# Linear attention and a gated feed-forward layer on one core: the first batch's q, v and all weights loaded in one row by GpSimd, and ScalarE's side work moved behind the output evictions

## The chip, the cores and the metric

The kernel runs on one core of a Trainium2 chip. Its time is the device time in microseconds, as the median of several runs: 335.98 before the change (3 runs, 335.76 to 336.26). One execution was taken with the hardware profiler; all times inside the kernel are from that one and count from the start of its span.

## The reference

Eight batches, eight heads, 576 positions, head size 64. First an attention without softmax: relu of q and k, each times a cosine and a sine of the position, so that the feature size doubles to 128; kv is the sum over positions of k's features times v, z the sum of k's features; the output is q's features times kv, divided by q's features times z.

```python
def phi(x, c, s):
    r = np.maximum(x, 0.0)
    return np.concatenate([r * c, r * s], axis=-1)
kv = np.einsum('bhsf,bhsd->bhfd', phi(k), v)
z = np.sum(phi(k), axis=2)
num = np.einsum('bhsf,bhfd->bhsd', phi(q), kv)
den = np.einsum('bhsf,bhf->bhs', phi(q), z)[..., None] + 1e-06
x = (num / den)             # laid out as 4608 tokens of 512
xn = x / sqrt(mean(x * x) + 1e-06) * rms_g
out = (silu(xn @ w_gate) * (xn @ w_val)) @ w_out     # 512 -> 1536 -> 512
```

Inputs and output are float32.

## The kernel before

**Tiles.** A batch's 576 positions are four tiles of 128 and half a tile; the half tiles of two batches make one tile. So there are nine blocks of 512 tokens: block b is the four full tiles of batch b, block 8 the four shared tiles. In a block the feed-forward runs in twelve steps (`step`, L626): in each, TensorE makes one bank of gate products (`gps`) and one of value products (`vps`), ScalarE takes silu of the first (`sil`, L647), VectorE multiplies (`hT`, L653). In blocks 0 to 4 a step takes fewer columns of more weight tiles, so that it can start before all four tiles of the block are there. From block 2 on each step also runs four of the 48 output matmuls of the block before (`out_mm`, L438): twelve of them fill the single bank `acc`, so that every third step ends with ScalarE's copy of that bank to SBUF (`osb`, L452) and two stores on SP's queue. Block 0's output matmuls are spread through `lead` (L663), between block 0 and block 1, where batch 1's attention is prepared.

**Attention work** is laid between the steps by a plan written by hand: `at(g, slot, function)` puts a piece into a slot of step g, and `step` runs the slots in the order sp, act0, dve0, gate matmuls, mid, value matmuls, silu, act1, dve1, product, output matmuls, pe. Every engine runs its instructions in program order, so a slot fixes what stands ahead of what on each engine's queue. The chain for one tile is: features of q and k (`feat`, L226, on DVE or ACT), a turn of q's features (`q_turn`, L281, a DMA transpose on SP, or on TensorE by `q_turn_pe` with an eviction `rqT`), `kv_mm` (L262) with its eviction `kvm`, `num_mm` (L309), `divide` (L335: three operations on DVE), `sumsq` (L353: a square with a sum on ACT, then the power -1/2 on GpSimd, `rs`, L361), `norm` (L364, `xn`, DVE), and a turn of `xn` into `xnT`, on TensorE by `x_turn_pe` (L380) with the eviction `x_evict` (L387).

**The opening**, before block 0, is written out at L722 to L763 and runs this chain for batch 0, with dummy matmuls (`warm_up`) between. A load of a tensor of a batch (`load`, L92) is two DMAs, of the even and the odd partitions; `cuts` splits it by columns. Batch 0's loads all go on SP's queue, in the order k, q(0:2), v(0:2), v(2:5), the norm's weights gb, q(2:5). The weights go on GpSimd's queue, which converts them to bf16: `load_gv(c)` loads a third of w_gate and w_val, `load_wo(c)` a third of w_out. Ahead of the first of them stands `pool_after` (L222), a copy on GpSimd of one element of v's first cast, so that the queue goes on only when that cast is done. The third `load_gv` comes later in the opening; `more_loads` (L516), in step 3, issues w_out and the k, q and v of batches 1 and 2, all on GpSimd's queue. GpSimd also computes each tile's `rs`, in order with its DMA issues.

```python
def load(t, src, b, odd_five=False, cuts=(0, NC5)):
    if b == 0:
        eng = nc.sync
    else:
        eng = nc.scalar if b > 2 and src is not v else nc.gpsimd
```

Of the kernel before, what the change touches and what calls it, by code (L numbers as in the profile page):

```python
# [11 lines left out]
BF16 = mybir.dt.bfloat16  # L12
# [5 lines left out]
def kernel(  # L18
# [11 lines left out]
    nc = tc.nc  # L30
    B, H, S, D = q.shape
    DM = H * D
    DFF = moe_w_gate.shape[1]
    P = 128
# [6 lines left out]
    NC5 = J + 1  # L41
# [5 lines left out]
    def K(i):  # L47
        tc.keep_in_program_order(i)
        return i

    consts = ctx.enter_context(tc.tile_pool(name="consts", bufs=1))
# [31 lines left out]
    def lanes(odd_five):  # L83

        if odd_five:
            return ((0, 0, J), (1, J, NC5))
        return ((1, NC5, J), (0, 0, NC5))

    def load(t, src, b, odd_five=False, cuts=(0, NC5)):  # L92
        if b == 0:
            eng = nc.sync
        else:
            eng = nc.scalar if b > 2 and src is not v else nc.gpsimd
        for lo, hi in zip(cuts[:-1], cuts[1:]):
            for par, t0, jn in lanes(odd_five):
                z = min(hi, jn)
                K(eng.dma_start(  # L100
                    out=t[par:P:2, :, lo * D : z * D],
                    in_=src[b, :, :, :].rearrange("h (i j) d -> i h (j d)", j=NT)[
                        :, :, (t0 + lo) * D : (t0 + z) * D
                    ],
                ))

    def load_v(b, cuts=(0, NC5)):
        load(vraw[b], v, b, False, cuts)

    def load_k(b):  # L110
        load(kraw[b], k, b)

    def load_q(b, cuts=(0, NC5)):
        load(qraw[b], q, b, b % 2 == 1, cuts)
# [3 lines left out]
    clear_fifth(v0, nc.vector)  # L118
    gb = consts.tile([P, DM], FP32, name="gb")
    load_k(0)  # L120
    load_q(0, (0, 2))
    load_v(0, (0, 2, NC5))
    K(nc.sync.dma_start(
        out=gb[:, :], in_=moe_rms_g.rearrange("(o d) -> o d", o=1).to_broadcast([P, DM])
    ))
    load_q(0, (2, NC5))


    iota_i = consts.tile([P, 1], mybir.dt.int32, name="iota_i")
# [1 line left out]
    odd_i = consts.tile([P, 1], mybir.dt.int32, name="odd_i")  # L131
    row_i = consts.tile([P, J], mybir.dt.int32, name="row_i")
    nc.gpsimd.iota(row_i[:, :], pattern=[[1, J]], base=0, channel_multiplier=0)
    iota_f = consts.tile([P, 1], FP32, name="iota_f")
    odd_f = consts.tile([P, 1], FP32, name="odd_f")
    row_f = consts.tile([P, J], FP32, name="row_f")
# [2 lines left out]
        out=odd_i[:, :], in_=iota_i[:, :], scalar=1, op=ALU.bitwise_and  # L139
# [10 lines left out]
        out=iota_f[:, :], in0=iota_f[:, :], scalar1=J + 0.5, scalar2=None, op0=ALU.mult  # L150
    )
    for u, half in ((0, 0.5), (1, -0.5)):
        nc.vector.scalar_tensor_tensor(
            out=first[:, u : u + 1], in0=odd_f[:, :], scalar=half, in1=iota_f[:, :],
# [3 lines left out]
            out=th[:, 1, u * J : (u + 1) * J], in0=row_f[:, :],  # L158
# [3 lines left out]
        out=th[:, 1, 2 * J : NT], in0=first[:, 1:2],  # L162
# [3 lines left out]
        out=th[:, 0, :], in_=th[:, 1, :], scalar=math.pi / 2.0, op=ALU.add  # L166
# [7 lines left out]

    ident_b = consts.tile([P, P], BF16, name="ident_b")
    masks.make_identity(nc, ident_b[:, :])
    mhalf = consts.tile([P, 1], FP32, name="mhalf")
    nc.gpsimd.memset(mhalf[:, :], -0.5)

# [5 lines left out]
    vx = [consts.tile([P, H, E], BF16, name=f"vx{j}") for j in range(NC5)]  # L185
# [15 lines left out]
    wg = consts.tile([P, NDT, DFF], BF16, name="wg")  # L201
    wv = consts.tile([P, NDT, DFF], BF16, name="wv")
    wo = consts.tile([P, NNT, DM], BF16, name="wo")
    probe = consts.tile([1, 1], BF16, name="probe")
    NG = 3
    GC = DFF // NG
    n4 = NNT // NG
# [1 line left out]
    def load_gv(c):  # L209
        for (w, src) in ((wg, moe_w_gate), (wv, moe_w_val)):  # L210
            K(nc.gpsimd.dma_start(
                out=w[:, :, c * GC : (c + 1) * GC],
                in_=src[:, c * GC : (c + 1) * GC].rearrange("(t p) n -> p t n", p=P),
            ))

    def load_wo(c):
        K(nc.gpsimd.dma_start(
            out=wo[:, c * n4 : (c + 1) * n4, :],
            in_=moe_w_out[c * n4 * P : (c + 1) * n4 * P, :].rearrange("(t p) m -> p t m", p=P),
        ))  # L220

    def pool_after(src):  # L222
        K(nc.gpsimd.tensor_copy(out=probe[:, :], in_=src))


    def feat(dst, src, scale, act):  # L226
# [99 lines left out]
    def xn_block(blk):  # L326
        if blk not in xnT:
            tag = "xnT" if blk < B else "xnTr"
            pool = xntp if blk < B else consts
            xnT[blk] = pool.tile([P, NDT, TB], BF16, name=tag, tag=tag)  # L330
        return xnT[blk]
# [55 lines left out]
    def x_evict(key, blk, col, dve=False):  # L387
        dst, src = xn_block(blk)[:, :, col * P : (col + 1) * P], xps.pop(key)[:, :, :]
        if dve:
            K(nc.vector.tensor_copy(out=dst, in_=src))  # L390
        else:
            K(nc.scalar.copy(out=dst, in_=src))  # L392
# [37 lines left out]
    def out_store(blk, jt, osb):  # L430
        if blk < B:
            rows = list(out_rows(blk, jt))
        else:
            rows = [r for o in range(2) for r in out_rows(2 * jt + o, J)]
        for par, dst in rows:
            K(nc.sync.dma_start(out=dst, in_=osb[par:P:2, :]))

    def out_mm(blk, i, tail=False):  # L438

        jt, nn = divmod(i, NNT)  # L440
        if nn == 0:
            if tail and jt % 2 == 0:
                acc[blk] = ps_gv.tile([P, DM], FP32, name="acc2", tag="gv")
            else:
                acc[blk] = ps_acc.tile([P, DM], FP32, name="acc", tag="acc")
        K(nc.tensor.matmul(  # L446
            acc[blk][:, :], lhsT=hT[blk][:, nn, jt * P : (jt + 1) * P], rhs=wo[:, nn, :],
            start=(nn == 0), stop=(nn == NNT - 1),
        ))
        if nn == NNT - 1:  # L450
            osb = osbp.tile([P, DM], FP32, name="osb", tag="osb")
            K(nc.scalar.copy(out=osb[:, :], in_=acc[blk][:, :]))  # L452
            out_store(blk, jt, osb)
# [6 lines left out]
    def at(g, w, f, *a):  # L460
        plan[g, w].append(lambda: f(*a))
# [13 lines left out]
    def feat_at(g, f, b, j, act):  # L475
        for c in range(2):
            on_act = c == 1 and act
            at(g, "act1" if on_act else "dve0" if f == k_feat else "dve1", f, b, j, c, on_act)

    def q_at(g, b, t, act=False):  # L480
        feat_at(g, q_feat, b, t, act)
        if t < J:
            at(g, "dve1", q_turn, b, t)

    def k_at(g, b, j, act=False):
        feat_at(g, k_feat, b, j, act)
# [26 lines left out]
        at(3, "dve1", q_feat, 0, J, c)  # L513


    def more_loads():  # L516
        for c in range(NG):
            load_wo(c)
        load_k(1)
        load_q(1, (0, 2))  # L520
        load_v(1)
        load_q(1, (2, NC5))
        load_k(2)
        load_q(2)
        load_v(2)

    at(3, "pe", more_loads)

    def pe_tile_at(g, key, xblk, col, gx):

# [7 lines left out]
    def q2_at(g, b, t):  # L538
        for c in range(2):
            at(g, "act1" if c else "dve1", q_feat, b, t, c, c == 1)  # L540
        if t < J:
            at(g, "dve1", q_turn, b, t)


    at(12, "dve0", divide, (1, 2))
# [64 lines left out]
    def run(g, w):  # L610
        for f in plan[g, w]:
            f()
# [13 lines left out]
    def step(blk, nn):  # L626
        g = blk * NNT + nn
        run(g, "sp")
        run(g, "act0")
        run(g, "dve0")  # L630
        while late_turns:
            x_turn(*late_turns.pop(0))
        if nn == 0:
            hT[blk] = htp.tile([P, NNT, TB], BF16, name="hT", tag="hT")
        if blk in PARTS:
            n0, c0, cn = PARTS[blk][nn]
            ni = TB // cn
            gp = gv_mm_part(wg, "gps", blk, n0, c0, cn)
            run(g, "mid")
            vp = gv_mm_part(wv, "vps", blk, n0, c0, cn)  # L640
            dst = hT[blk][:, n0 : n0 + ni, c0 : c0 + cn]
        else:
            gp = gv_mm(wg, "gps", blk, nn)
            vp = gv_mm(wv, "vps", blk, nn)
            dst = hT[blk][:, nn, :]
        sil = silp.tile([P, TB], BF16, name="sil", tag="sil")
        K(nc.scalar.activation(out=sil[:, :], in_=gp[:, :], func=AF.Silu))  # L647
        run(g, "act1")
        run(g, "dve1")
        a, c = vp[:, :], sil[:, :]  # L650
        if blk in PARTS:
            a, c = (z.rearrange("p (i n) -> p i n", i=ni) for z in (a, c))
        K(nc.vector.tensor_tensor(out=dst, in0=a, in1=c, op=ALU.mult))  # L653
        if blk > 1:
            for i in range(4 * nn, 4 * nn + 4):
                out_mm(blk - 1, i)
        run(g, "pe")

    def outs(lo, hi):
# [74 lines left out]
    for j in range(NC5):  # L734
        v_cast(0, j, act=(j == 3))
        kv_mm(0, j, j == 0, j == NC5 - 1)
        if j == 0:
            pool_after(vx[0][0:1, 0, 0:1])
            load_gv(0)
            load_gv(1)  # L740
        if j == 1:
            warm_up(5)
    kv_evict(0)
# [13 lines left out]
    num_mm((0, 2))  # L757
    q_feat(0, 3, 0, act=True)
    x_turn_pe((0, 0))
    x_evict((0, 0), 0, 0)  # L760
    load_gv(2)
    divide((0, 2))
    norm((0, 1))  # L763

# [55 lines left out]
```

## Time and profile before

| | us | |
|---|---|---|
| median of the runs | 335.98 | 335.76 to 336.26 |
| the profiled execution | 337.09 | its time as a run |
| its span | 334.9 | first to last instruction |
| TensorE busy (matmul) | 318.3 | 95% of the span |
| VectorE (DVE) busy | 190.2 | 57% |
| ScalarE (ACT) busy | 169.2 | 51% |
| GpSimd (POOL) busy | 47.9 | 14% |
| gate and value matmuls of the feed-forward start | 20.3 | first `gps` |
| DMA | 50.63 MB | mean 151 GB/s |

The chain that ended last is TensorE for 80% of the span and DMA for 7%. The granted TensorE clock is full in every slice but the last. The GB/s count what is written to the destination; weights and v of batches 1 to 7 are read as float32 and written as bf16, so they read twice what they show.

To read a line of the timeline: start, duration, engine, source line, operation, the tile written and the tiles read, the shape, how many were merged, and in brackets how long the engine had stood idle and what released it. PEld is TensorE's weight load; SPq, ACTq and POOLq are DMA issues by these engines.

### The profile page before, as it was taken

The page shows a single profiled execution, that of the slowest core. Times are in us where ns is not written, and L with a number is a line of the kernel's source. Part 1 is how long each engine was busy: PE and PEld are TensorE (multiplying, and loading weights), DVE is VectorE, ACT ScalarE, POOL GpSimd, SP SyncE. Part 2 cuts the span into 40 slices and gives each one's busy share as a digit, 9 for nine tenths or more (in the row PEclk, how much of TensorE's full clock was granted, in tenths as well). Part 3 has the DMA queues.
Part 4 walks back from the last instruction along what each step waited for, and adds up shares of the span by engine and source line. Part 5 has one row for each costly group of instructions (what it writes and reads, how often), then busy time and mean ns, then how long its engine had stood idle before and what let it go on. Part 6 is the DMA issues. An engine that isn't in the chain of part 4 may idle for free.

```text
span 334.9 us, 7537 instructions
## 1 busy us (share of the span) xinstructions
PE 318.3 (95%) x3009; PEld 213.4 (64%) x3045; DVE 190.2 (57%) x394; ACT 169.2 (51%) x320; POOL 47.9 (14%) x91
## 2 busy tenths in 40 slices
PE   6679999998999999999999999999999999999995
PEld 4568856996887788778877744454444444444443
DVE  5676476776866575588857686665652422222300
ACT  3764377775875447486646474644433322233221
POOL 3446361300012120031103001000100000000000
PEclk9999999999999999999999999999999999999999
DMA  7999999893239989999969994253123021000012
GB/s 219 273 205 184 229 296 348 228 234 95 65 96 197 239 202 169 283 272 202 167 120 237 291 165 110 65 142 80 47 65 94 32 65 46 34 33 31 31 63 96
DMA packets 82147, 50.63 MB, mean 151 GB/s; under 512 B 49056, under 2 KB 76464, under 8 KB 82112
## 3 DMA queue, kind: packets, MB, share of 16 engines
q1 hardware_dynamic: 58032, 24.65, 33.8%
q0 software_dynamic: 13360, 13.57, 22.7%
q10 hardware_dynamic: 10720, 11.93, 12.2%
q8 instruction: 24, 0.39, 0.5%
q14 instruction: 11, 0.09, 0.1%
HBM read 38.01 MB, written 9.44 MB: 142 GB/s over the span
## 4 chain that ended last, share of the span: by engine, by line
PE 80%; DMA 7%; DVE 5%; ACT 4%; issue 2%; ACTq 1%; POOL 1%; SPq 0%; DVEq 0%
PE acc L446 25%; PE gps L401 12%; PE vps L401 12%; PE gps L414 12%; PE vps L414 12%; DMA rqT<-qp 3%; PE att L316 3%; DMA wv<-in_moe_w_val_dram 3%; PE att L267 2%; DMA kbuf<-in_k_dram 2%; DVE kp L231 1%; ACT kp L229 1%; PE qtp L294 1%; DVE xn L366 1%; PE acc L781 1%
## 5 line engine op out<-in xcount | busy, mean ns | idle before, releaser
L653 DVE TENSOR_TENSOR hT<-vps,sil 128x512 bf16<-128x512 f32 x108 | 74.5, 690 | 98.9 <-PE vps L401 59.6
L647 ACT ACTIVATE sil<-gps 128x512 bf16<-128x512 f32 x108 | 64.5, 597 | 109.6 <-PE gps L401 61.9
L446 PE MATMUL acc<-wo,hT 128*128 128x512 bf16 x395 | 101.8, 379 | 1.9 <-ACT osb L452 0.6
L446 PEld LDWEIGHTS <-hT 128*128 128x128 bf16 x420 | 40.0, 98 | 40.5 <-issue 0.9
L414 PE MATMUL gps<-xnT,wg 128*128 128x128 bf16 (+1 forms) x704 | 62.7, 239 | 0.7 <-ACT xnT L392 0.7
L414 PE MATMUL vps<-xnT,wv 128*128 128x128 bf16 (+1 forms) x704 | 62.8, 239 | 0.5 <-DMA wv<-in_moe_w_val_dram 0.5
L414 PEld LDWEIGHTS <-wg 128*128 128x128 bf16 x704 | 50.2, 98 | 6.8 <-DMA wg<-in_moe_w_gate_dram 0.6
L414 PEld LDWEIGHTS <-wv 128*128 128x128 bf16 x704 | 51.3, 98 | 3.8 <-DMA wv<-in_moe_w_val_dram 0.7
L361 POOL TENSOR_TENSOR rs<-ss,mhalf 128x1 f32<-128x1 f32 x36 | 20.1, 559 | 200.1 <-ACT sq L356 200.0
L401 PE MATMUL gps<-xnT,wg 128*128 128x512 bf16 x139 | 36.7, 379 | 0.4
L401 PE MATMUL vps<-xnT,wv 128*128 128x512 bf16 x141 | 36.5, 379 | 0.1
L452 ACT COPY osb<-acc 128x512 f32<-128x512 f32 x35 | 20.4, 583 | 26.4 <-PE acc L446 21.8
L401 PEld LDWEIGHTS <-wv 128*128 128x128 bf16 x192 | 18.8, 98 | 22.7
L366 DVE SCALAR_TENSOR_TENSOR xn<-x,rs,gb 128x512 bf16<-128x512 f32 x36 | 26.9, 748 | 8.8 <-POOL rs L361 8.8
L401 PEld LDWEIGHTS <-wg 128*128 128x128 bf16 x192 | 18.0, 98 | 20.1
L345 DVE TENSOR_TENSOR x<-att,rec 128x512 f32<-128x512 f32 x36 | 24.9, 691 | 1.2
L231 DVE TENSOR_SCALAR kp<-kbuf,trig 128x512 bf16<-128x512 f32 x50 | 22.8, 489 | 3.1 <-DMA kbuf<-in_k_dram 2.7
L231 DVE TENSOR_SCALAR qp<-qbuf,trig 128x512 bf16<-128x512 f32 x52 | 23.9, 485 | 0.4 <-DMA qbuf<-in_q_dram 0.4
L356 ACT ACTIVATE sq<-x 128x513 f32<-128x513 f32 x36 | 22.6, 626 | 2.9 <-DVE x L345 2.5
L229 ACT ACTIVATE kp<-kbuf,trig 128x512 bf16<-128x512 f32 x30 | 20.6, 712 | 3.4 <-DMA kbuf<-in_k_dram 3.4
L316 PEld LDWEIGHTS <-rqT 128*128 128x128 bf16 x320 | 14.3, 98 | 9.1 <-issue 1.1
L229 ACT ACTIVATE qp<-qbuf,trig 128x512 bf16<-128x512 f32 x28 | 19.6, 714 | 0.4 <-DMA qbuf<-in_q_dram 0.4
(63 smaller groups left out, 193.2 us busy)
## 6 DMA issues: line engine op xcount, KB each, us to landing
out_dram<-osb SPq DMA_DIRECT2D x70, 128.0 KB, 2.6
kbuf<-in_k_dram ACTq DMA_DIRECT2D x5, 640.0 KB, 6.1
qbuf<-in_q_dram ACTq DMA_DIRECT2D x5, 640.0 KB, 8.2
kbuf<-in_k_dram ACTq DMA_DIRECT2D x5, 512.0 KB, 4.8
qbuf<-in_q_dram ACTq DMA_DIRECT2D x5, 512.0 KB, 6.5
vbuf<-in_v_dram POOLq DMA_DIRECT2D x7, 320.0 KB, 9.4
vbuf<-in_v_dram POOLq DMA_DIRECT2D x7, 256.0 KB, 6.7
wg<-in_moe_w_gate_dram POOLq DMA_DIRECT2D x3, 512.0 KB, 10.1
```

The source lines that it names most:

```text
L229: K(nc.scalar.activation(out=dst, in_=src, func=AF.Relu, scale=scale))
L231: K(nc.vector.tensor_scalar(out=dst, in0=src, scalar1=scale, scalar2=0.0, op0=ALU.mult, op1=ALU.max,))
L316: K(nc.tensor.matmul(nums[key][:, h // Z, (h % Z) * E : (h % Z) * E + D + 1], lhsT=rqT[a, t][:, h, :], rhs=kvm[a % NK][:, h, 0 : D + 1], s ...
L345: K(nc.vector.tensor_tensor(out=x[:, 0:DM].rearrange("p (z s d) -> p z s d", z=2, d=D), in0=a[:, :, :, 0:D], in1=r.unsqueeze(3).to_broadca ...
L356: K(nc.scalar.activation(out=sq[:, :], in_=xs[key][:, :], func=AF.Square, scale=1.0 / math.sqrt(DM), accum_out=ss[:, :],))
L366: K(nc.vector.scalar_tensor_tensor(out=xn[:, :], in0=xs.pop(key)[:, 0:DM], scalar=rss.pop(key)[:, :], in1=gb[:, :], op0=ALU.mult, op1=ALU. ...
L401: K(nc.tensor.matmul(ps[:, :], lhsT=w[:, dt, nn * P : (nn + 1) * P], rhs=xnT[blk][:, dt, :], start=(dt == 0), stop=(dt == NDT - 1),))
L414: K(nc.tensor.matmul(ps[:, i * cn : (i + 1) * cn], lhsT=w[:, dt, (n0 + i) * P : (n0 + i + 1) * P], rhs=xnT[blk][:, dt, c0 : c0 + cn], star ...
L446: K(nc.tensor.matmul(acc[blk][:, :], lhsT=hT[blk][:, nn, jt * P : (jt + 1) * P], rhs=wo[:, nn, :], start=(nn == 0), stop=(nn == NNT - 1),))
L452: K(nc.scalar.copy(out=osb[:, :], in_=acc[blk][:, :]))
L647: K(nc.scalar.activation(out=sil[:, :], in_=gp[:, :], func=AF.Silu))
L653: K(nc.vector.tensor_tensor(out=dst, in0=a, in1=c, op=ALU.mult))
```

## The change

Four things:

- Batch 0's q and v and the norm's weights gb go to GpSimd's queue; only k stays on SP's. On GpSimd's queue the order is q(0:2) after two iotas, v after the identity matrix, then (behind the other constants) q(2:5), gb, all three thirds of w_gate and w_val and two thirds of w_out. The copy that held the queue back is gone.
- The last third of w_out and batch 1's k are issued in step 0, batch 1's q and v in step 2, batch 2's in step 3.
- In the steps from block 2 on that end with an output eviction, ACT's slot act1 runs after the output matmuls and their eviction, not ahead of them. So that a turn of q by DMA still follows its features in program order, these turns move from slot dve1 to slot pe.
- The eviction of the first turned tile of the opening, `x_evict((0, 0), 0, 0)`, goes from ACT to DVE.

```diff
     def load(t, src, b, odd_five=False, cuts=(0, NC5)):
-        if b == 0:
+        if b == 0 and src is k:
             eng = nc.sync
         else:
             eng = nc.scalar if b > 2 and src is not v else nc.gpsimd
...
     load_k(0)
-    load_q(0, (0, 2))
-    load_v(0, (0, 2, NC5))
-    K(nc.sync.dma_start(
-        out=gb[:, :], in_=moe_rms_g.rearrange("(o d) -> o d", o=1).to_broadcast([P, DM])
-    ))
-    load_q(0, (2, NC5))
...
     nc.gpsimd.iota(row_i[:, :], pattern=[[1, J]], base=0, channel_multiplier=0)
+    load_q(0, (0, 2))
...
     masks.make_identity(nc, ident_b[:, :])
+    load_v(0, (0, 2, NC5))
...
-    def pool_after(src):
-        K(nc.gpsimd.tensor_copy(out=probe[:, :], in_=src))
+    load_q(0, (2, NC5))
+    K(nc.gpsimd.dma_start(
+        out=gb[:, :], in_=moe_rms_g.rearrange("(o d) -> o d", o=1).to_broadcast([P, DM])
+    ))
+    for c in range(NG):
+        load_gv(c)
+    for c in range(2):
+        load_wo(c)
...
     def q_at(g, b, t, act=False):
         feat_at(g, q_feat, b, t, act)
         if t < J:
-            at(g, "dve1", q_turn, b, t)
+            at(g, "pe", q_turn, b, t)
...
-    def more_loads():
-        for c in range(NG):
-            load_wo(c)
-        load_k(1)
-        load_q(1, (0, 2))
-        load_v(1)
-        load_q(1, (2, NC5))
-        load_k(2)
-        load_q(2)
-        load_v(2)
-
-    at(3, "pe", more_loads)
+    at(0, "pe", load_wo, 2)
+    at(0, "pe", load_k, 1)
+    for f, *a in ((load_q, 1, (0, 2)), (load_v, 1), (load_q, 1, (2, NC5))):
+        at(2, "pe", f, *a)
+    for f in (load_k, load_q, load_v):
+        at(3, "pe", f, 2)
...
     def q2_at(g, b, t):
         for c in range(2):
             at(g, "act1" if c else "dve1", q_feat, b, t, c, c == 1)
         if t < J:
-            at(g, "dve1", q_turn, b, t)
+            at(g, "pe", q_turn, b, t)
...
         K(nc.scalar.activation(out=sil[:, :], in_=gp[:, :], func=AF.Silu))
-        run(g, "act1")
+        ends = blk > 1 and nn % 3 == 2
+        if not ends:
+            run(g, "act1")
         run(g, "dve1")
...
                 out_mm(blk - 1, i)
+        if ends:
+            run(g, "act1")
         run(g, "pe")
...
-        if j == 0:
-            pool_after(vx[0][0:1, 0, 0:1])
-            load_gv(0)
-            load_gv(1)
...
     x_turn_pe((0, 0))
-    x_evict((0, 0), 0, 0)
-    load_gv(2)
+    x_evict((0, 0), 0, 0, dve=True)
     divide((0, 2))
     norm((0, 1))
```

More of the change, by code (lines that the diff above doesn't have):

```diff
@@ L203 @@
     wo = consts.tile([P, NNT, DM], BF16, name="wo")
-    probe = consts.tile([1, 1], BF16, name="probe")
     NG = 3
```

## The prediction

> **What bounds the kernel now.** I read the busy shares first, then TensorE's waits by stretch, then the timeline of the places where it waits. Times are us from the span's start, in one profiled execution: span 334.9, time 337.09. The median is 335.98, so 1.11 lower than that execution; I work out a difference from the trace and apply it to the median. A timeline line gives start, duration, engine, line, operation and tiles; in brackets the idle time before it and what ended that.
>
> ```profile
> PE 318.3 (95%) x3009; PEld 213.4 (64%) x3045; DVE 190.2 (57%) x394; ACT 169.2 (51%) x320; POOL 47.9 (14%) x91
> ```
>
> TensorE is the bound. The change can win only where TensorE idles, or where the opening delays its stream. The waits view from 84 us on shows one releaser for TensorE, two output evictions of 0.6 us together; the larger is
>
> ```profile
> 140.70 1.02 PE L446 MATMUL acc<-wo,hT 128*128 128x512 bf16 x4 [0.38 <-ACT osb L452]
> ```
>
> From 60 to 84 it idles 1.5 us (a DMA transpose, a norm): neither the transposes' issue step there nor the loads beside them move. From 44 to 60 it idles 0.85 us, in the lead to block 1. The rest is the opening: the first gate matmuls start at 20.30.
>
> ```profile
> 1.56 5.61 DMA kbuf<-in_k_dram
> 12.96 1.01 DVE L243 CAST vx<-v 128x512 bf16<-128x512 f32 x2 [0.43 <-DMA v<-in_v_dram]
> 19.67 0.58 ACT L392 COPY xnT<-xps 128x512 bf16<-128x512 bf16 x1 [0.29 <-PE xps L384]
> 20.13 0.74 DVE L366 SCALAR_TENSOR_TENSOR xn<-x,rs,gb 128x512 bf16<-128x512 f32 x1
> 20.30 1.05 PE L414 MATMUL gps<-xnT,wg 128*128 128x128 bf16 x16 [0.67 <-ACT xnT L392]
> 22.06 1.07 PE L414 MATMUL vps<-xnT,wv 128*128 128x128 bf16 x16 [0.48 <-DMA wv<-in_moe_w_val_dram]
> ```
>
> k lands at 1.56 + 5.61 = 7.17; from there a chain of features, turns, casts, kv, num, divide, sumsq and norm runs with one DMA wait, 0.43 for v, until xnT is evicted at 20.25. The weights are late only for the first vps, by 0.48. So the gate costs half a microsecond, not the 12 us it stands for.
>
> **The change, part by part.**
>
> *Loads of q and v to GpSimd's queue.* k's two DMAs keep their issue times (0.74, 1.56). In the trace's single-packet records SP's q and v go in packets of 512 bytes at 291 GB/s (8 to 10 us); GpSimd's loads of the same form (q, k of batches 1 and 2) go in packets of about 4096 bytes at 351 (49 to 51 us). q(0:2) and v are 0.52 + 1.18 = 1.70 MB: 5.8 us at the one rate, 4.9 at the other, so v lands about 0.9 earlier and the 0.43 goes. Next late is the evictor itself (DVE casts back to back), so the gain is no more than 0.43: **-0.43**, bounds -0.43 and 0.
>
> The Trainium skill ("DMA: Bandwidth & Descriptors", Issuing engines are not separate DMA queues) says that DMAs from different engines share the same 16 engines and only issue time is saved. By it v would land no earlier, this term would be 0 and the sum -0.41; the two rates above speak against it.
>
> *Does k suffer?* k now shares the engines with q. Nearest row: at 120.20 and 120.85 ACT issues a k load, at 121.55 GpSimd a v load.
>
> ```profile
> 120.20 0.61 ACTq L100 DMA_DIRECT2D kbuf<-in_k_dram  x1
> 120.85 0.65 ACTq L100 DMA_DIRECT2D kbuf<-in_k_dram  x1
> 121.55 1.50 POOL L100 DMA_DIRECT2D vbuf<-in_v_dram  x2
> ```
>
> In the packet records v's first packet comes at 125.5, when k is nearly through (126); without such a load ahead GpSimd's first packet comes 2.0 after issue (65.26 to 67.25). The later queue waited for what was queued earlier. GpSimd can issue q at 1.0, after two iotas (0.84, 0.93), so it arrives near 3.0, between k's first DMA (2.5) and its second (about 3.2). I take **0**, as in that row. Upper bound: q and all of v go ahead of k, 1.70 MB at 0.35 MB/us = +4.9.
>
> *GpSimd's own line.* Ahead of the first rs (L361, 17.79 in the trace, wanted at 17.36 after the 0.43) now stand 17 DMA issues and 2.8 us of setup (0.84 to 3.64). Issues last 0.69 to 0.91: 17 times that is 11.7 to 15.5, so GpSimd is free at 15.5 to 19.3; with the typical 0.76 (the gate loads' later issues) at 16.7, which is hidden by 0.6. Price 0, upper bound +1.9. GpSimd also has at most 8 DMAs in flight:
>
> ```profile
> 36.33 0.69 POOL L100 DMA_DIRECT2D vbuf<-in_v_dram  x1 [1.65 <-DMA wo<-in_moe_w_out_dram]
> ```
>
> that is the 15th, waiting for the 7th. So the 17th waits for the 9th, gb: q, k, v and gb are 3.8 MB, through by about 14.5, before the 15.9 at which the 17th comes up. The first wg is the 10th and needs only the second q piece; it lands near 17, wv near 19.5 (512 KB written at 205 GB/s is 2.6 each), and the 0.48 at vps goes.
>
> *x_evict((0,0)) to DVE.* DVE takes it at 19.63 for 0.42 (its other xnT copies), ACT took 0.58. It now stands ahead of divide((0,2)), whose three operations took 1.12, and norm((0,1)) comes after both: 19.63 + 0.42 + 1.10 + 0.74 = 21.9 in place of 20.87. The turn of that norm is queued on TensorE ahead of vps, so vps starts at 21.9 + 0.4 = 22.3 in place of 22.06: what the gone weight wait frees, this wait takes. Net **+0.24**; bounds 0 and +0.7. What follows on TensorE (q_turn, gps of step 1) shifts with it.
>
> *Lead.* Without the pause between v and weights the row of loads ends about 2.6 earlier (wv at 19.5 against 22.0).
>
> ```profile
> 45.00 2.56 ACT L229 ACTIVATE kp<-kbuf,trig 128x512 bf16<-128x512 f32 x4 [0.98 <-DMA kbuf<-in_k_dram]
> 48.71 0.62 PE L294 MATMUL qtp<-ident_b,qp 128*128 128x128 bf16 x8 [0.56 <-DVE qp L231]
> ```
>
> ACT's 0.98 goes: four features, the eviction and the first q feature come earlier, q's turn is then bound by DVE's feature (47.71 + 0.48 = 48.19). TensorE gains 48.71 - 48.25: **-0.45**, bounds 0 and -0.8. DVE gains nothing, since its hT ends at 45.06.
>
> *ACT's extra work behind the evictions.* The two waits of 0.38 and 0.20 go: -0.58. In return sumsq((2,3)) in step 26 starts behind the eviction, some 0.75 into step 27; sumsq 0.82, rs 0.63 and norm 0.75 bring its turn to 3.0, where TensorE comes at 2.6: +0.4. Elsewhere the work behind is up to 2.2 us, and silu then ends about when its bank is wanted (three banks, two steps ahead). **-0.2**, bounds -0.58 and +0.5. Turning q on SP moves behind the step's stores; the users come 3 to 8 steps later (about 8 us or more, a transpose lands in 3.9): 0.
>
> Sum: -0.43 + 0 + 0.24 - 0.45 - 0.2 = **-0.84**: 335.98 - 0.84 = **335.1**.
>
> **The rivals.**
>
> *Packets take turns, and k pays (slower).* For: at 74.5 to 75.5 SP's 256-byte and ACT's 1280-byte packets run side by side, 115 against 114, then 121 against 119. The Trainium skill (same page, Queues, rings and completion order) states it as the rule: each engine goes round its queues packet by packet. Against: the row at 120. If it holds from the start, each 1024 or 1280 bytes of k go beside 4096 of q and v. With only q(0:2) and half of v ahead, 1.05 MB at 0.35, k lands 3.0 later: 338.1; with all of v 340. It makes the kernel slower once k is over 1.5 late (-0.84 + 1.5 = +0.66). Chance 0.18.
>
> *GpSimd's line becomes the bound (slower).* At 0.85 to 0.91 per issue the first rs is late by 1.0 to 1.9 and the whole opening with it: 336.1 to 337.0. For: the first two weight issues took 0.91 and 0.86. Against: the other four took 0.75 to 0.78, later plain loads 0.69. Chance 0.15, nearly all of it slower.
>
> *The wins are hidden.* One q piece (0.26 MB, 0.75 us) goes ahead of k's second DMA, or v lands no earlier; the eviction on DVE takes back the weight wait: 335.6 to 335.9, within 0.2%. The first wv, the 11th, can't be issued before the first v piece has landed, so a gate of a kind stays. Chance 0.25.
>
> *The forecast*, chance 0.42. 0.2% is 0.67 us, about what a measurement of this kernel can tell from no change. The forecast gives faster 0.42, the hidden case same 0.25 with 0.03 of the second rival, the rest slower 0.30. Range: 333.9 (osb's full 0.58, and DVE's order costs nothing) to 338.2 (the first rival's first price); about 0.1 lies above, some below.
>
> **What would show it.** k's features starting at 7.3 (over 8.7 is the first rival); v's cast without a wait; the first rs following its sumsq by 0.1 (else GpSimd's line); vps of step 0 waiting for DVE's xn, not for wv; k features of the lead without a DMA wait on ACT; no osb wait on TensorE after 84. I am wrong if the first gps starts over 1 us away from 20, or if new waits show in the blocks behind.

## The result, and the profile after

The changed kernel takes 339.15 us (median of 4 runs, 338.55 to 339.99) against 335.93 (335.76 to 336.26) for the kernel before, taken again on the same chip: a ratio of 1.0096, 95% interval 1.0070 to 1.0122. On a second chip (the run e9 below) it was 1.0045 (1.0011 to 1.0078). The medians are those of all runs; the ratios, their intervals and the groups of runs further down leave out the few runs that lie more than 1.5% above the fastest of the same kernel (one each in e2, e8 to e11 and e13, two in e15). So the change is slower by 0.5 to 1%, and the forecast of 335.1 was wrong, range included. The profiled execution of after took 339.57 with a span of 337.4, that of before 337.09 and 334.9: 2.5 us more, which is what the traces have to account for.

The page's busy times of after, to be held against those of before:

```profile
PE 321.2 (95%) x3045; PEld 214.3 (64%) x3045; DVE 188.8 (56%) x395; ACT 168.6 (50%) x319; POOL 54.7 (16%) x99
```

TensorE is again busy for 95%, and with 2.9 us more of it (a part of that is records missing in the page of before: 3009 matmuls, not 3045). The same work lasting longer is a first hint that TensorE itself was slower somewhere. The timeline of after's opening (start, duration, engine, line, operation, tiles; in brackets the idle time before and what ended it):

```profile
1.40 1.55 POOL L101 DMA_DIRECT2D qbuf<-in_q_dram  x2 [0.35 <-issue]
4.15 2.75 POOL L101 DMA_DIRECT2D v<-in_v_dram  x4
9.38 2.56 ACT L231 ACTIVATE kp<-kbuf,trig 128x512 bf16<-128x512 f32 x4 [4.21 <-DMA kbuf<-in_k_dram]
12.69 1.58 PE L296 MATMUL qtp<-ident_b,qp 128*128 128x128 bf16 x16 [4.35 <-ACT qp L231]
14.06 1.91 PE L718 MATMUL wps<-warm 128*128 128x256 bf16 x8
15.77 0.97 PE L269 MATMUL att<-vx,kp 128*128 128x65 bf16 x16
18.08 0.60 ACT L279 CAST kvm<-att 128x520 bf16<-128x520 f32 x1 [2.24 <-PE att L269]
21.21 0.57 POOL L363 TENSOR_TENSOR rs<-ss,mhalf 128x1 f32<-128x1 f32 x1 [4.09 <-ACT sq L358]
23.57 1.05 PE L416 MATMUL gps<-xnT,wg 128*128 128x128 bf16 x16 [0.51 <-DVE xnT L392]
25.27 0.40 PE L386 MATMUL xps<-ident_b,xn 128*128 128x128 bf16 x4 [0.64 <-DVE xn L368]
25.50 1.06 PE L416 MATMUL vps<-xnT,wv 128*128 128x128 bf16 x16
```

The same places in the timeline of before:

```profile
10.51 1.23 PE L294 MATMUL qtp<-ident_b,qp 128*128 128x128 bf16 x16 [2.08 <-ACT qp L229]
11.58 1.04 PE L718 MATMUL wps<-warm 128*128 128x256 bf16 x8
12.45 0.67 PE L267 MATMUL att<-vx,kp 128*128 128x65 bf16 x16
14.66 0.59 ACT L277 CAST kvm<-att 128x520 bf16<-128x520 f32 x1 [1.10 <-PE att L267]
```

Two things stand in these lines. **k is late**: its features start at 9.38 on the word of k's DMA, 2.09 later than before (7.29). The second of k's DMAs, issued at the same time as before, lands near 9.3 and not at 7.17. **TensorE is slow for a while**: q's first turn comes 2.18 later (12.69 against 10.51), but `kvm` 3.42 later (18.08 against 14.66). The 1.24 in between is not in any wait. It is in the durations: the same 16 turns took 1.58 and not 1.23, the same 8 dummy matmuls 1.91 and not 1.04, the first 16 matmuls of kv 0.97 and not 0.67. The table of busy times by stretch gives the clock that was granted (after, then before; the columns are the stretch, its length, busy time of PE, PEld, DVE, ACT and POOL with counts, granted clock, DMA share, GB/s):

```profile
8.40:12.60 4.20, 0.00 (x0) 0.00 (x0) 3.20 (x8) 3.23 (x6) 4.20 (x6) 1.00 1.05 305
12.60:16.90 4.30, 4.21 (x43) 3.65 (x44) 2.74 (x6) 2.09 (x3) 4.30 (x6) 0.60 1.11 259
```

```profile
8.40:12.60 4.20, 2.12 (x30) 1.84 (x30) 3.52 (x9) 3.49 (x6) 0.34 (x2) 1.00 1.16 310
12.60:16.90 4.30, 3.21 (x67) 2.58 (x63) 2.09 (x6) 2.67 (x5) 3.16 (x4) 1.00 1.14 235
```

After's TensorE does nothing in the first stretch (x0): the 34 dummies of `warm_up`, which were to cover the wait for k, end at 8.34 and k's features are not even begun. Then the clock is 0.60. The Trainium skill ("TensorE: Matmul & The Clock Gate", What's actually happening) says that the clock falls to half after an idle window of about 3.4 us, in a window that runs freely, and comes back after as much work. After's pause of 4.35, the half clock that its record shows from 13.04 for 3.41 us, and the 8 dummies at 1.91 against 1.04 agree with it; other pauses follow below, and not all of them agree.

From `kvm` on, after runs as before did, 3.3 to 3.5 later, and wins a part back. The shift of VectorE's product of step n (`hT`, after minus before) is 3.48 in step 0, 3.45 in step 6, 2.89 in step 12, 3.07 in step 21, and 2.6 from step 60 to the end. The waits of TensorE from 84 us on, in after, no longer name `osb`:

```profile
PE xps L386 <- DVE xn L368: 0.7, 1, 0.7
PE gps L403 <- DMA xnT<-xn: 0.2, 1, 0.2
```

### The profile page after: what moved, and what is told of

The parts are those of the page before. It is cut to its first block, busy times and chain, and to the rows that moved or that the text cites. A ratio compares the mean times of both kernels' runs of the same rounds, so it can differ in the third digit from the quotient of the medians.

```text
span 337.4 us, 7568 instructions
## 1 busy us (share of the span) xinstructions
PE 321.2 (95%) x3045; PEld 214.3 (64%) x3045; DVE 188.8 (56%) x395; ACT 168.6 (50%) x319; POOL 54.7 (16%) x99
## 4 chain that ended last, share of the span: by engine, by line
PE 82%; DMA 8%; DVE 3%; ACT 3%; issue 2%; POOL 1%; SPq 0%; ACTq 0%; DVEq 0%
PE acc L448 26%; PE gps L403 12%; PE vps L403 12%; PE vps L416 12%; PE gps L416 12%; DMA rqT<-qp 3%; PE att L318 3%; PE att L269 2%; DMA kbuf<-in_k_dram 2%; DMA xnT<-xn 2%; PE qtp L296 1%; DVE xn L368 1%; PE xps L386 1%; ACT sq L358 1%; ACT kp L231 1%
## 5 line engine op out<-in xcount | busy, mean ns | idle before, releaser
L448 PE MATMUL acc<-wo,hT 128*128 128x512 bf16 x420 | 105.7, 379 | 0.0
L363 POOL TENSOR_TENSOR rs<-ss,mhalf 128x1 f32<-128x1 f32 x36 | 20.9, 580 | 207.0 <-ACT sq L358 207.0
```

The lines of the kernel that those rows point to most:

```text
L363: K(nc.gpsimd.tensor_tensor(out=rs[:, :], in0=ss[:, :], in1=mhalf[:, :], op=ALU.pow))
L448: K(nc.tensor.matmul(acc[blk][:, :], lhsT=hT[blk][:, nn, jt * P : (jt + 1) * P], rhs=wo[:, nn, :], start=(nn == 0), stop=(nn == NNT - 1),))
```

## The experiments

The theory after this profile had two parts: (1) k lands late because q and v of GpSimd's queue now share the DMA engines with it; (2) the longer pause then lowers TensorE's clock, and that adds to it. The rivals were that (1) is GpSimd's late and long line, and not the sharing, that (2) is chance, and that the other edits (ends, `x_evict`, loads in steps 0 to 3) cost something as well. All ratios are against the kernel before on the same chip in the same session, with 95% intervals; "after" and "before" in a heading say what the kernel was made from. A run's granted clock is the mean over its whole span.

**e1: after, with 58 dummies ahead of the first turn** (part 2).

```diff
-    warm_up(34)
+    warm_up(58)
```

> The changed kernel with 58 opening dummy matmuls in place of 34, so that TensorE is busy until q's first turn (they end at about 12.3 in place of 8.34). Theory: besides k's lateness (landed 9.26 against 7.17) the changed kernel loses 1.2 us because TensorE stood idle for 4.35 us and its granted clock was 0.60 from 12.6 to 16.9. Then the clock stays at 1.00, the first gate matmuls start at about 22.4 in place of 23.57, and the time falls by 1.2 to 337.9. Rival: the extra comes from GpSimd's 17 issues beside VectorE's casts; then nothing changes (339.1) whatever the clock.

Measured: 336.23, 0.9997 (0.9975 to 1.0020), every run at a clock of 0.998 or more. Its timeline:

```profile
8.25 2.56 ACT L231 ACTIVATE kp<-kbuf,trig 128x512 bf16<-128x512 f32 x4 [3.09 <-DMA kbuf<-in_k_dram]
11.48 1.23 PE L296 MATMUL qtp<-ident_b,qp 128*128 128x128 bf16 x16 [0.33 <-ACT qp L231]
12.55 1.04 PE L718 MATMUL wps<-warm 128*128 128x256 bf16 x8
```

With the pause at 0.33 the dummies take 1.04 and kv follows at full speed: part 2 holds. It gave more than was expected (337.9); in this profile k's features also began 1.1 earlier than in after's, for which the edit has no reason (k's landing varies between executions: 9.38, 8.91 in e9, 8.82 in e15, 8.25 here).

**e2: after, with k ahead of q on GpSimd's queue** (part 1: in one queue there is no sharing).

```diff
-        if b == 0 and src is k:
-            eng = nc.sync
-        else:
-            eng = nc.scalar if b > 2 and src is not v else nc.gpsimd
+        eng = nc.scalar if b > 2 and src is not v else nc.gpsimd
```

> The changed kernel with k too on GpSimd's queue, as the first of the row. Theory: k was late because its packets of 1024 and 1280 bytes took turns with q's and v's of 4096 on another queue; in one row nothing goes beside it, and 1.18 MB at 0.3 MB/us from about 3.0 land at 7.0 to 8.0, the features start at 7.2 to 8.0, TensorE's pause is 1.5 us shorter, and the time is 336.0 to 337.0. Rival: GpSimd's loads are slow in themselves, or the engines' total rate is the limit; then k lands at 9 or later and the time is 339 or more.

Measured: 338.75, 1.0046 (1.0030 to 1.0062). k's features began at 7.69, so k alone behaved as part 1 said; the time did not, and for part 2's reason:

```profile
12.04 1.87 PE L293 MATMUL qtp<-ident_b,qp 128*128 128x128 bf16 x16 [2.98 <-DVE qp L230]
13.70 1.91 PE L715 MATMUL wps<-warm 128*128 128x256 bf16 x8
```

The turn came 4.35 after the start of k's features (before: 3.22), since DVE's six of them took 3.79 in place of 2.6; the pause was 2.98, and turns and dummies ran slow. The gate and value matmuls were slow once more at 24 to 28 us (1.26 and 1.91 for 16, against 1.05): the granted clock halves again at 24.76, though no pause in the 3.4 us before it is longer than 0.88. Why DVE's features took longer stays open.

**e3: before, with 8 dummies** (part 2 without any of the change).

```diff
-    warm_up(34)
+    warm_up(8)
```

> The kernel before with 8 opening dummy matmuls in place of 34: they end at about 4.2, so TensorE stands idle for 6 us until q's first turn at 10.5, while k lands as before at 7.17. Theory: the granted clock drops to about 0.6 around 10.5 to 14.5 and turns, dummies and kv run slower: 1.0 to 1.3 us on the path, 337.1. Rival (the clock costs nothing on this path): 335.9.

Measured: 345.9, 1.0267 (1.0229 to 1.0305). The sign is right, the size is not:

```profile
10.38 1.89 PE L294 MATMUL qtp<-ident_b,qp 128*128 128x128 bf16 x16 [5.67 <-ACT qp L229]
12.06 1.91 PE L718 MATMUL wps<-warm 128*128 128x256 bf16 x8
22.36 1.67 PE L414 MATMUL gps<-xnT,wg 128*128 128x128 bf16 x16 [0.67 <-ACT xnT L392]
84.07 0.62 PE L316 MATMUL att<-kvm,rqT 128*128 128x65 bf16 x8 [3.81 <-DMA rqT<-qp]
```

k was as early as before (its features at 7.15), and the pause alone made `kvm` 2.06 late (16.72 against 14.66). The clock fell again before the first gate matmuls (1.67 against 1.05), which made 3.0 at the end of block 0. The rest, up to 9.8 at the end of the span, came later: 3.8 of it is the DMA transpose that TensorE waited for at 84 (before waits 0.8 for one there), with half the clock again behind it (from 84.05 for 3.41 us); 2.4 are waits for `osb` (before: 0.6). Why these waits came is open; so e3 shows the direction and the first 3 us, and not that a clock loss costs 10.

**e4: before, without the copy that holds the weights back** (part 1 in before's own opening: weights on GpSimd against v on SP).

```diff
         if j == 0:
-            pool_after(vx[0][0:1, 0, 0:1])
             load_gv(0)
```

> The kernel before without the copy that holds GpSimd's queue back; q and v stay on SP. The first two thirds of the gate and value weights are then issued from about 3.6 and written in packets of 1024 bytes beside q's and v's of 512. Theory (packets take turns): q and v, 1.7 MB, share the engines with 2 MB of weights and v lands 3 us or more later (16 in place of 12.9), k hardly; 338 to 340. Rival (what was queued earlier goes first): v lands within 0.5 of before, the weights by 17, and the time is 335.4 to 335.9.

Measured: 347.19, 1.0309 (1.0292 to 1.0326), far more than the 338 to 340 expected.

```profile
6.96 2.56 ACT L229 ACTIVATE kp<-kbuf,trig 128x512 bf16<-128x512 f32 x4 [2.01 <-DMA kbuf<-in_k_dram]
14.23 0.76 DVE L243 CAST vx<-v 128x512 bf16<-128x512 f32 x2 [2.69 <-DMA v<-in_v_dram]
21.82 0.76 DVE L243 CAST vx<-v 128x512 bf16<-128x512 f32 x2 [6.83 <-DMA v<-in_v_dram]
```

The weights were issued from 3.60 on, but their first packet came only at 8.44. k, through by 6.3, landed as before; v, all of it issued by 7.6, was complete 8.9 later (the last casts at 21.82, before 12.96). In the packet records from 10 to 15 us, each microsecond holds 136 to 147 of the weights' packets (1024 bytes written, twice that read) and 130 to 148 of v's of 512 bytes. So two queues that have work at the same time take turns packet by packet, and the one with small packets loses far more than half: v moved at some 72 GB/s in place of 290. The prediction said that the gate costs half a microsecond and saves nothing that shows; with q and v on SP it is worth some 10 us, a part of which is the half clock that TensorE then had from 17.49 for 13.65 us.

**e5, e6, e7: the other edits alone, in before.**

```diff
 # e5: q_turn in slot pe, and act1 behind the evictions
+        ends = blk > 1 and nn % 3 == 2
+        if not ends:
+            run(g, "act1")
...
 # e6
-    x_evict((0, 0), 0, 0)
+    x_evict((0, 0), 0, 0, dve=True)
...
 # e7: e5, and the loads in steps 0, 2 and 3 as in after, with before's opening and copy
+    for c in range(NG):
+        at(0, "pe", load_wo, c)
+    at(0, "pe", load_k, 1)
...
```

> The kernel before with one part of the change alone: ACT's slot act1 behind the output eviction in the steps that end with one (and q's DMA turns moved to slot pe). The forecast priced it at -0.2; in the changed kernel's trace TensorE's waits for osb are gone and the shift against before falls by 0.5 after 84 us, with one wait of 0.7 for a norm added. Expected: -0.3 to -0.5, 335.6 to 335.8 on a kernel before of 336.1 (ratio 0.9985 to 0.9991), no osb wait on TensorE. Rival (the moved work gives back what it frees): ratio 1.000.

> The kernel before with the first x_evict on DVE alone. The forecast priced it at +0.24 with the wait for wv gone; here the weights stay late (wv lands at 22.0), so that vps starts at max(22.1, 22.3): +0.2 to +0.3, ratio 1.0006 to 1.001, and vps waits for DVE's xn, not for wv. Rival (the earlier xnT wins more than the later norm costs): ratio under 1.

> The kernel before with the change's later parts and its own opening: act1 behind the evictions, w_out and batch 1's k issued in step 0, batch 1's q and v in step 2, batch 2's in step 3; k, q, v and gb on SP, the copy, and x_evict on ACT as before. Theory: the changed kernel's loss lies in the opening alone, and its later parts win -0.45 in the lead and -0.4 behind it: -0.8, ratio 0.9975, no wait for k's DMA in the lead. Rival (the later parts lose too, or the lead's gain needs the earlier row of weights): ratio 0.999 or more.

Measured: e5 336.22, 0.9986 (0.9969 to 1.0002); e6 336.28, 0.9983 (0.9969 to 0.9997); e7 335.92, 0.9982 (0.9966 to 0.9999). None of them costs anything, so the loss is all in the opening. Nor can any of them be told from nothing: e6, expected to lose a little, and e14 below, expected to win next to nothing, read 0.998 as well. In e5's trace TensorE waits for nothing from 84 on (before: 0.6 for `osb`), and its last steps are 0.87 earlier. In e6 `vps` waits for `xn`, as expected, but `kvm` to `vps` takes 7.43, before 7.40: without the earlier weights DVE's order costs next to nothing there, not 0.2 to 0.3. e7 is 0.87 ahead of before by step 12: 0.37 of it stands in step 0 already, in an opening that the edit leaves as it was (`vps` waits 0.34 for `wv`, before 0.48), and 0.5 comes in the lead, where no k wait is left. But in its profile TensorE waited 2.5 for two DMA transposes of q (before: 0.8 for one), and nothing is left at the end (+0.07).

**e8: after, with q and v issued behind GpSimd's constants** (part 1: a later arrival; q issued at 3.60 in place of 1.40, v at 5.14 in place of 4.15; and 40 dummies).

```diff
     nc.gpsimd.iota(row_i[:, :], pattern=[[1, J]], base=0, channel_multiplier=0)
-    load_q(0, (0, 2))
...
     masks.make_identity(nc, ident_b[:, :])
-    load_v(0, (0, 2, NC5))
...
         clear_fifth(t, nc.gpsimd)
+    load_q(0, (0, 2))
+    load_v(0, (0, 2, NC5))
...
-    warm_up(34)
+    warm_up(40)
```

> The changed kernel with q and v issued behind GpSimd's constants (from 3.6 in place of 1.4) and 40 dummies in place of 34. Theory: k was late by 1 to 2 because q's first pieces arrived at 4.0 between k's two DMAs; issued at 3.6 they arrive at about 5.6, k lands by 7.5, the dummies end at 9.3, less than 2.2 before q's first turn, no matmul of the opening is slow, and the time is 0.8 to 1.2 under the kernel before (ratio 0.9965 to 0.9977). Rival (k's late part waits for any load of the other queue, or q and v now come too late): k at 8.5 or later, or v's cast waiting, and a ratio of 1.000 or more.

Measured: 335.35, 0.9972 (0.9950 to 0.9994).

```profile
3.60 1.55 POOL L101 DMA_DIRECT2D qbuf<-in_q_dram  x2
7.06 2.56 ACT L231 ACTIVATE kp<-kbuf,trig 128x512 bf16<-128x512 f32 x4 [2.15 <-DMA kbuf<-in_k_dram]
10.43 1.09 PE L296 MATMUL qtp<-ident_b,qp 128*128 128x128 bf16 x16 [0.50 <-DVE qp L233]
19.79 1.05 PE L416 MATMUL gps<-xnT,wg 128*128 128x128 bf16 x16 [0.52 <-DVE xnT L392]
```

This is the deciding run. The queues, packets and bytes are those of after, and k is as early as before: in the packet records q's first packet comes at 6.04, when 1.13 of k's 1.18 MB have been started (in after at 4.26, with 0.40 started). The gate matmuls start 3.8 earlier than in after. So a transfer suffers from another queue's packets that arrive while it still has its own to move. That its own were issued first does not save it: v's were, in e4.

**e9 to e11: after again, and with 40 and 46 dummies** (how steady is part 2, and how many dummies it takes).

```diff
-    warm_up(34)
+    warm_up(40)     # e10; 46 in e11; e9 is after itself
```

> The changed kernel itself, on the same chip as the next three, since its first time came from another chip and one profile of it had k at 9.26, while the same kernel with 58 dummies had k at 8.13. Theory: ratio 1.008 to 1.010 as before; k lands anywhere from 8 to 9.3 and the first matmuls after the pause run slow. Rival (the first time was a chip's own): ratio under 1.004.

> The changed kernel with 40 dummies in place of 34: they end at about 9.3 and TensorE's pause before q's first turn is 2.3 to 3.4 us, as k lands. Theory: a pause of up to 2.4 left the matmuls fast and one of 2.98 or more made them slow in the runs so far, so this one lies at the edge: times of both kinds, between 336.2 and 339, with a wide spread. Rival (the pause does not matter, only k): the same ratio as the changed kernel's.

> The changed kernel with 46 dummies: they end at about 10.3, the pause is 1.3 to 2.4 us. Theory: below the edge; eight dummies take 1.04 and not 1.91, the time is that with 58 dummies, a ratio of 0.999 to 1.001. Rival (the pause does not matter, or the extra dummies win in another way): the changed kernel's ratio, or one that goes on falling with the number of dummies.

Measured: e9 338.39, 1.0045 (1.0011 to 1.0078); e10 338.10, 1.0021 (0.9986 to 1.0056); e11 337.51, 1.0015 (0.9984 to 1.0046). e9 was expected at 1.008 to 1.010 and e11 at 0.999 to 1.001; both missed. In each of the three the runs fall into two groups by their clock (in e11 the times of the two overlap): at 0.998 or more 336.25 to 337.60 (e9), 336.11 to 336.40 (e10), 336.07 to 338.53 (e11); below it 337.78 to 340.63, 336.96 to 341.05, 337.03 to 338.68. All four runs of after in the first measurement were below 0.996. The traces say what such a reading is: every half-clock stretch that they record inside a span lasts 3.41 us, or two or four times that (6.83 in e2 and e13, 13.65 in e4), and one of 3.41 lowers the mean over 335 us by 0.005. So 0.995 is one such stretch, and 0.998 or more is none before the last microseconds. So part 2 is a matter of the single run: 2 of 10 runs were at 0.998 or more with 34 dummies, 3 of 10 with 40, 6 of 10 with 46, all 10 of e1 with 58. e9's profiled execution is one that was spared: a pause of 3.31, then 8 dummies in 1.04. With the dummies alike, only q's and v's place differs between e10 and e8 (40 dummies: 1.0021 against 0.9972) and between e11 and e16 below (46: 1.0015 against 0.9944).

**e12, e13, e16: e8 with the first `x_evict` on ACT (e12), that with 46 dummies (e13), and e8 with 46 dummies (e16)**, to see what DVE's eviction costs once the weights are early, and what is best.

```diff
-    x_evict((0, 0), 0, 0, dve=True)
+    x_evict((0, 0), 0, 0)
```

> The kernel with q and v behind the constants and 40 dummies (ratio 0.9972), with the first x_evict back on ACT. With wv there in time, the forecast says that DVE's eviction puts norm((0,1)) ahead of vps and costs 0.24; alone in the kernel before it cost nothing (0.02 by the distance from kvm to vps). Forecast's step: 0.2 to 0.5 faster, vps starting without a wait 7.0 after kvm in place of 7.4. Rival (ACT's later sumsq and silu take it back): no difference, 0.997.

> q and v behind GpSimd's constants, the first x_evict on ACT, and 46 dummies in place of 40, so that the pause before q's first turn is under 1 us. With 40 the runs fell in two groups, 333.7 to 334.3 at a mean clock of 0.998 or more and 335.1 to 335.4 at 0.993 to 0.998. Theory: only the first group is left: 333.9, ratio 0.992, clock 0.998 or more in all runs. Rival (the groups have another cause): both groups again.

> The changed kernel with q and v behind GpSimd's constants and 46 dummies: clock full, k at 7.1 to 7.3, the first x_evict on DVE. Theory: e15 minus k's lateness: 1 to 2 us under it, ratio 0.994 to 0.996; and 0.3 to 0.6 over e13 for DVE's eviction. Rival: as e15.

Measured: e12 335.06, 0.9935 (0.9907 to 0.9963); e13 335.17, 0.9931 (0.9912 to 0.9951); e16 335.08, 0.9944 (0.9928 to 0.9960). In e12's timeline:

```profile
20.14 1.05 PE L416 MATMUL gps<-xnT,wg 128*128 128x128 bf16 x16 [0.67 <-ACT xnT L394]
21.28 1.07 PE L416 MATMUL vps<-xnT,wv 128*128 128x128 bf16 x16
```

`vps` follows `gps` with no wait, 6.79 behind `kvm` against 7.42 in e8: with the weights in time, DVE's order costs 0.6 at that place, and e12's products stay 0.3 to 0.5 ahead of e8's from step 0 to the last. These are the best versions found, 0.6 to 0.7% faster than before by their ratios (of which some 0.2% is what e6 and e14 read too); between e12, e13 and e16 the intervals do not decide. 46 dummies did not remove the lower clock readings, against what was expected of e13 (three of its six runs are at 0.995), so not every one of them comes from this pause.

**e14 and e15: before with 46 dummies, after with 58 once more** (controls, on the chip of e13 and e16).

```diff
-    warm_up(34)
+    warm_up(46)     # e14, in before; 58 in e15, in after
```

> The kernel before with 46 dummies. Its pause was 2.1 and nearly all its runs (80 of 84 with a reading) had a clock of 0.997 or more. Theory: nothing to win, ratio 0.9985 to 1.000. Rival (the kernel before loses to the clock as well, so that the dummies' win in the changed kernel says nothing of the change): ratio 0.996 or less.

> The changed kernel with 58 dummies, on the chip of e16: clock full, k late (8.1 to 9.3). Theory: k's 1 to 2 us eat the later parts' gain of about 1: ratio 0.999 to 1.003, so that of the changed kernel's loss in its first runs (1.0096) some two thirds were the clock's. Rival (k's lateness costs nothing at full clock): the ratio of e16.

Measured: e14 336.48, 0.9982 (0.9969 to 0.9996); e15 338.65, 1.0043 (1.0012 to 1.0074), above its range. Before gains next to nothing from dummies: with its pause of 2.08, 103 of the 105 runs of before beside these experiments read a clock of 0.997 or more. e15 is not e1 again: six of its runs, at 0.998 or more, take 336.43 to 337.63, four, at 0.993 to 0.995, take 339.67 to 340.95. What lowered the clock of these four is open: the profiled run's pause of 1.46 would not have, by the rows above.

Two traces show that the opening is not the only place for it. TensorE waited 3.81 at 80.3 us in e3 and 4.73 at 147.4 in e13 (a profiled execution of 341.55) for a DMA transpose of q, and the granted clock is half from 84.05 for 3.41 in the one, from 151.00 for 6.83 in the other. The waits for these transposes sum to 0 to 2.5 in the other profiles, so they change from execution to execution. The runs with the lower clock are 0.9 (e16), 1.4 (e12) to 3.6 us (e15) above the others of their kernel, by the groups' medians; since one stretch of 3.41 us at half clock takes at most 1.7 from TensorE, the larger of these gaps must hold waits as well, and none of them can be read as the price of the clock alone.

k's lateness can be separated from the clock. At 0.998 or more, e15 takes 336.77 (median of 6) and e16 334.71 (of 4). Their traces differ by 1.14 in step 0 and by 1.65 at the end; the 0.5 between comes in steps 18 to 21, where e15 waits 0.3 for a DMA transpose of q and e16 does not. After at full clock (e9) is 1.87 behind e8 in step 0. So **k's lateness alone costs about 1.1 to 1.9 us** in the opening.

## Why the prediction was wrong, step by step

- **"Does k suffer? I take 0": the step that failed.** Its nearest row (ACT's k loads at 120.20 and 120.85, GpSimd's at 121.55) was one in which both k loads were issued ahead of the other queue, and there the later queue's packets came behind. In the opening q's first packet came at 4.26 (the prediction had "near 3.0"), when 0.40 of k's 1.18 MB had been started. In after's packet records, by half microseconds: from 4.5 to 5.0, 43 of q's packets of 4096 bytes go beside 34 of k's 1024 and 3 of its 1280; from 5.0, 16 of q's beside 63 of k's; from 5.5 to 6.5 k goes all but alone; from 7.0, 33 of GpSimd's next beside 33 of k's; from 7.5, 29 beside 21; from 8 to 9 the last 8 of k. k lands 2.1 late. This is the first rival (0.18), whose price for q(0:2) and half of v was 3.0. Its point of decision, k over 1.5 late, was passed, and so was the prediction's own sign of being wrong: the first `gps` starts at 23.57, over 1 us from 20. In the row at 120 v's first packet came 3.8 after its issue, with k nearly through, so that the two hardly met; whether it waited for k is open, and in e4 the later queue did not wait for v. (On the trace's clock the rival's row at 74.5 reads 122 packets against 118, then 163 against 108: turns, but less even ones.) The Trainium skill ("DMA: Bandwidth & Descriptors", Queues, rings and completion order) was right that an engine goes round its queues by packets; e4 and after agree for queues that both have work, e8 agrees in that there is next to nothing to share with a queue whose packets come when k is through.
- **Cover by dummies, priced at nothing.** No term asked what else hangs on k. With k at 7.2 the 34 dummies left a pause of 2.08, with k at 9.3 one of 4.35, and the clock falls: 1.24 of the 3.42 at `kvm` in that execution. No rival held it either. That is why the measured 339.15 lies above the range, and above the first rival's 338.1; e9's two runs at full clock, 336.25 and 337.60, lie inside it.
- **v, -0.43.** The cast has no wait any more, as foreseen, but only because k made everything else later; in e8, with k in time and v issued 1.0 later than in after, it waits 0.27. The rate was 291 to 322 GB/s (145 to 161 KB in each half microsecond from 9 to 12), not 351.
- **GpSimd's line, 0 (bound +1.9).** Right: the weights' last issue ended at 17.1, and the first `rs` at 21.21 follows its sum. e8 shows it with k in time: the last weight's issue ends at 16.50 and the first `rs` starts at 17.43, on its sum's word, with 0.93 to spare. (The prediction's sums here run 0.1 to 0.2 high: from 3.64, 17 issues of 0.76 end at 16.6.)
- **`x_evict` on DVE, +0.24.** Right in kind: `vps` waits for `xn` (0.64) and not for `wv`. Its price is hidden in before (e6: 0.02) and is 0.5 to 0.6 with early weights (e8 against e12). e12 shows that the change need not have this loss.
- **Lead, -0.45.** Right: k's features at 47.37 without a wait, the shift goes from 3.45 to 2.89, -0.56.
- **Work behind the evictions, -0.2.** Right in sign, too small: `osb`'s waits of 0.58 are gone, one norm wait and a DMA transpose of 0.9 together came, and the shift goes from 3.07 in step 21 to 2.61 at the end, -0.46. As a time alone it can't be told from nothing (e5, 0.9986, up to 1.0002). The 3.9 that the prediction took for a transpose to land was a median; the longest of q's took 11.7 in before.
- **"The wins are hidden", 0.25.** Its condition (one q piece ahead of k, 0.75) was too small by 1.3.

The sum by what the traces show, as shifts of after against before: k and the turn behind it +2.18, the slow clock up to `kvm` +1.24, from there to block 0's end +0.03, lead -0.56, steps 12 to 21 +0.18 (a DMA transpose that TensorE waits for, 1.0 in place of 0.8), from there to the last step -0.46: +2.61, of which the span shows 2.5. The parts behind `kvm` came out near the forecast; the opening decided.

## What to carry to other kernels

Keep the load that everything waits for alone until it is nearly through: let a second queue start so late that its first packets arrive behind it, above all when that queue moves bigger packets, and read when they arrive, not when they are issued. Where TensorE waits for such a load, fill the whole wait with dummy matmuls and leave slack: in these runs pauses of 2.98 us and more, with one exception, turned a late load into a late load and a slow TensorE. A gate that looks idle in a profile may be what keeps two queues apart, so price it by what would run together without it, not by the wait that it causes.

## What the runs showed of the hardware that was not expected

- **Packet size decides who gets the engines.** GpSimd's loads without a conversion go in packets of about 4096 bytes (up to 5120 for k in e2), SP's of the same tensors in 512 to 1280. In e4, where the weights' packets write 1024 bytes and read twice that, they took turns with v's of 512 one for one and held v back from 12.9 to 21.8.
- **The clock's edge is near 3 us and not sharp, and one long pause is not needed.** Pauses and the speed behind them, from single profiles: 2.08 (before), 2.41 in e4 at another place, and 3.31 (e9) stay fast; 2.98 (e2), 4.35 (after) and 5.67 (e3) are slow, with 8 dummies at 1.91 against 1.04. By the granted clock, TensorE was busy for 0.00 to 1.79 us of the 3.41 us ahead of each recorded fall inside a span (after 0.35; e2 1.36 and 1.79; e3 1.63 and 0.00; e4 1.30; e13 0.00). A window that runs freely, as the Trainium skill has it (the page and section cited above), would make an edge of that kind; but a window with 1.79 us of matmuls is not an idle one, so less than the idle window that it names was enough here.
- **The clock in the trace is not always the clock.** In e3, 8 dummies took 1.91, so half speed, in a stretch whose granted clock reads 1.00; the length of a known matmul is the better witness:

```profile
10.00:16.00 6.00, 5.62 (x53) 4.77 (x54) 2.90 (x7) 2.46 (x4) 3.40 (x5) 1.00 1.09 263
```

- **From issue to arrival.** GpSimd's first packets came 1.8 to 4.8 us after the start of the issue (65.26 to 67.07 in before, 3.60 to 6.04 in e8, 1.40 to 4.26 in after, 121.55 to 125.34 in before, 3.60 to 8.44 in e4). That delay, and not the order of issue, decided how much of k was left when q came. What sets it is open.
